# x + alpha * fx: a compact head for the first 23 columns of the flat tensors, and four stores instead of three

## The chip, the core and the metric

The kernel runs on one core of a Trainium2 chip. The metric is device time in microseconds (us); the figure for a kernel is the median of several runs. Beside it stands a profile of one execution, whose span runs from the first to the last recorded event on the core; what surrounds the span belongs to the run's time, but not to the profile.

## What is computed

```python
B, S, D = 512, 32, 640
x, fx   # (B, S, D) bf16
alpha   # (1,) bf16

def reference(x, fx, alpha):
    return x + alpha * fx
```

Both inputs and the output hold 512 x 32 x 640 = 10,485,760 bf16 numbers, 20.97 MB each.

## The kernel before

Each tensor is taken as a flat run of numbers and cut into 128 equal rows, one for each partition of the on-chip memory (lines 61 to 63). A row has 160 columns of K = 512 numbers, so a column is 1 KiB in a partition, a row is 160 KiB, and neighbouring rows begin 160 KiB apart in memory.

Three lists cut the columns into pieces. `X` cuts the loads of x: (0, 8), (8, 46), (46, 92), (92, 115), (115, 154), (154, 160). `F` cuts fx: six pieces of 23 columns and one of 22. `S` cuts the stores: 64, 64 and 32 columns. All of x lies in one tile, `x_t`, that is as large as the tensor; the pieces of fx share two buffers, `f_t`, so the third piece of fx can only be loaded when the first has been used.

The order of the work is written out by hand in `PLAN`: "x i" loads piece i of x, "f j" piece j of fx, "a" loads alpha and spreads it over the partitions, "c j" computes, "s i" stores. Every transfer is issued by SyncE (SP), on one queue, in the order of `PLAN` (`transfer`, line 78); an issue that has to wait holds back those behind it on SP. Step "c j" is two instructions on VectorE: piece j of fx times alpha, in place (line 96), and x plus that, in place in `x_t` (line 99). The step "a" has a tiny transfer, a 1x1 matmul against a row of ones (line 113) and a copy to all partitions (line 115).

`LATE` makes store 0 wait until the last piece of fx has landed, so that no store is issued ahead of the last loads. At the end a no-op on SP waits for everything but the last store (lines 123 to 125); the program's own end waits for that one.

In what follows, "f 2", "c 5" or "s 1" are steps of `PLAN`, numbered from 0, and a column is always 1 KiB in each of the 128 partitions.

Of the kernel before, what the change touches and what calls it, by code (L numbers as in the profile page):

```python
# [1 line left out]

# [4 lines left out]

ACT = mybir.ActivationFunctionType
ALU = mybir.AluOpType
F32 = mybir.dt.float32  # L10
BF16 = mybir.dt.bfloat16

K = 512
P = 128


X = [(0, 8), (8, 46), (46, 92), (92, 115), (115, 154), (154, 160)]
F = [(0, 23), (23, 46), (46, 69), (69, 92), (92, 115), (115, 138), (138, 160)]
S = [(0, 64), (64, 128), (128, 160)]
N = 160  # L20

PLAN = """
x 0
x 1
a
f 0
f 1
x 2
c 0
f 2  # L30
c 1
f 3
x 3
c 2
f 4
x 4
c 3
f 5
c 4
f 6  # L40
x 5
c 5
c 6
s 0
s 1
s 2
"""
LATE = {("s", 0): ("f", 6)}


@with_exitstack
def kernel(
    ctx: ExitStack,
    tc: tile.TileContext,
    x: bass.AP,
    fx: bass.AP,
    alpha: bass.AP,
    out: bass.AP,
):
    nc = tc.nc  # L60
    xv = x.flatten_outer_dims().rearrange("(p n) d -> p (n d)", p=P)
    fxv = fx.flatten_outer_dims().rearrange("(p n) d -> p (n d)", p=P)
    ov = out.flatten_outer_dims().rearrange("(p n) d -> p (n d)", p=P)
    assert xv.shape[1] == N * K

    consts = ctx.enter_context(tc.tile_pool(name="consts", bufs=1))
    psum = ctx.enter_context(tc.tile_pool(name="psum", bufs=1, space=bass.MemoryType.PSUM))
    whole = ctx.enter_context(tc.tile_pool(name="whole", bufs=1))
    fs = ctx.enter_context(tc.tile_pool(name="fs", bufs=2))
    ctx.enter_context(tc.manual_schedule())  # L70

    sync = mybir.DependencyInfo(mybir.DependencyClass.Sync, mybir.DependencyReason.DATA)
    xt = whole.tile([P, N * K], x.dtype, name="x_t")
    ft, moved = {}, {}
    done = []

    def transfer(what, out, in_):
        r = nc.sync.dma_start(out=out, in_=in_)  # L78
        if what in LATE:
            tc.add_manual_dep(r.ins, moved[LATE[what]].ins.name, sync, reason="issue late")  # L80
        moved[what] = r
        done.append(r)

    def load_x(i):
        a, b = X[i]
        transfer(("x", i), xt[:, a * K : b * K], xv[:, a * K : b * K])

    def load_f(j):
        a, b = F[j]
        ft[j] = fs.tile([P, max(e - s for s, e in F) * K], fx.dtype, tag="f", name="f_t")  # L90
        transfer(("f", j), ft[j][:, : (b - a) * K], fxv[:, a * K : b * K])

    def compute(j):
        a, b = F[j]
        term, total = ft[j][:, : (b - a) * K], xt[:, a * K : b * K]
        nc.vector.tensor_scalar(  # L96
            out=term, in0=term, scalar1=lanes["a_f"][:], scalar2=None, op0=ALU.mult
        )
        done.append(nc.vector.tensor_tensor(out=total, in0=total, in1=term, op=ALU.add))  # L99

    def store(i):
        a, b = S[i]
        transfer(("s", i), ov[:, a * K : b * K], xt[:, a * K : b * K])

    lanes = {}

    def alpha_to_lanes():
        a_1 = consts.tile([1, 1], alpha.dtype, name="a_1")
        transfer("a", a_1[:], alpha[None, :])
        ones = consts.tile([1, P], alpha.dtype, name="ones")  # L110
        nc.vector.memset(ones[:], 1.0)  # L111
        a_ps = psum.tile([P, 1], F32, name="a_ps")
        done.append(nc.tensor.matmul(a_ps[:], ones[:], a_1[:], start=True, stop=True))  # L113
        lanes["a_f"] = consts.tile([P, 1], F32, name="a_f")
        nc.vector.tensor_copy(out=lanes["a_f"][:], in_=a_ps[:])  # L115

    does = {"x": load_x, "f": load_f, "c": compute, "s": store, "a": alpha_to_lanes}
    for step in PLAN.split("\n"):
        if step:
            what, *of = step.split()  # L120
            does[what](*map(int, of))

    rest = nc.sync.nop(nofuse=True)
    for i in done[:-1]:
        tc.add_manual_dep(rest.ins, i.ins.name, sync, reason="all but the last store")


# [1 line left out]
_INS = ['x', 'fx', 'alpha']  # L129
_OUTS = [((512, 32, 640), 'bfloat16')]  # L130


# [23 lines left out]
```

## Time and profile before

| what | value |
|---|---|
| median of 3 runs | 151.09 us (151.03 to 151.19) |
| the profiled execution's own time | 151.26 us |
| its span | 149.5 us |
| VectorE: 7 multiplies (L96), 7 additions (L99) | 22.9 us, 43.8 us |
| HBM read, written | 41.94 MB, 20.97 MB |
| mean rate over the span | 421 GB/s |
| SP's issues of transfers | 0.33 to 0.64 us each |

How to read the profile: an engine's busy time is summed over its instructions, and the share is that of the span. DVE is VectorE, SP is SyncE, and SPq stands for SP's sequencer, which issues transfers. A line of the timeline gives start and duration in us, engine, line of the kernel, operation, what is written and read, and in brackets how long the engine had been idle and what ended that. A line of the list of transfers gives what is written and read, how many there are, their size in KB, and the us from issue to landing. A line of the windows gives a stretch of the span, its length, the busy time of each engine in it, the clock, the mean busy share of the 16 DMA engines, and the rate in GB/s; packets are booked where they start, so a short stretch can show more than 1.00.

### The profile page before, as it was taken

The page shows a single profiled execution, that of the slowest core. Times are in us where ns is not written, and L with a number is a line of the kernel's source. Part 1 is how long each engine was busy: PE and PEld are TensorE (multiplying, and loading weights), DVE is VectorE, ACT ScalarE, POOL GpSimd, SP SyncE. Part 2 cuts the span into 40 slices and gives each one's busy share as a digit, 9 for nine tenths or more (in the row PEclk, how much of TensorE's full clock was granted, in tenths as well). Part 3 has the DMA queues.
Part 4 walks back from the last instruction along what each step waited for, and adds up shares of the span by engine and source line. Part 5 has one row for each costly group of instructions (what it writes and reads, how often), then busy time and mean ns, then how long its engine had stood idle before and what let it go on. Part 6 is the DMA issues. An engine that isn't in the chain of part 4 may idle for free.

```text
span 149.5 us, 93 instructions
## 1 busy us (share of the span) xinstructions
PE 0.2 (0%) x1; PEld 0.1 (0%) x1; DVE 66.7 (45%) x16; POOL 0.2 (0%) x4
## 2 busy tenths in 40 slices
PE   0000000000000000000000000000000000000000
PEld 0000000000000000000000000000000000000000
DVE  0000005999950099999499104999960000000000
POOL 0000000000000000000000000000000000000000
DMA  5998999999979999999998999999996969696994
GB/s 151 463 500 354 448 410 466 435 403 466 542 303 410 466 435 403 429 460 422 443 502 353 417 460 390 458 515 438 403 561 281 561 281 561 281 561 281 456 456 210
DMA packets 2306, 62.92 MB, mean 421 GB/s; under 512 B 258, under 2 KB 258, under 8 KB 386
## 3 DMA queue, kind: packets, MB, share of 16 engines
q1 hardware_dynamic: 2306, 62.92, 98.2%
HBM read 41.94 MB, written 20.97 MB: 421 GB/s over the span
## 4 chain that ended last, share of the span: by engine, by line
DMA 41%; DVE 31%; issue 1%; SPq 1%; DVEq 0%
DMA f_t<-in_fx_dram 41%; DVE x_t L99 20%; DVE f_t L96 11%; SPq L78 1%; DVEq L96 0%
## 5 line engine op out<-in xcount | busy, mean ns | idle before, releaser
L99 DVE TENSOR_TENSOR x_t<-x_t,f_t 128x11776 bf16<-128x11776 bf16 (+1 forms) x7 | 43.8, 6254 | 0.2
L96 DVE TENSOR_SCALAR f_t<-f_t,a_f 128x11776 bf16<-128x11776 bf16 (+1 forms) x7 | 22.9, 3265 | 26.7 <-DMA f_t<-in_fx_dram 26.7
L115 DVE COPY a_f<-a_ps 128x1 f32<-128x1 f32 x1 | 0.2, 159 | 16.2 <-PE a_ps L113 16.2
L111 DVE MEMSET ones<- 1x128 bf16 x1 | 0.2, 165 | 0.8 <-PEq L140 0.8
L113 PE MATMUL a_ps<-a,ones 1*128 1x1 bf16 x1 | 0.2, 158 | 17.0 <-DMA a<-in_alpha_dram 17.0
L140 POOL MEMSET const-bfloat16-1.0<- 128x1 bf16 x1 | 0.1, 101 | 0.0
L140 POOL MEMSET const-uint8-127<- 128x1 uint8 x1 | 0.1, 101 | 0.0
L113 PEld LDWEIGHTS <-ones 1*128 1x128 bf16 x1 | 0.1, 98 | 1.0 <-DVE ones L111 1.0
L140 POOL MEMSET const-float32-0.0<- 128x1 f32 x1 | 0.1, 98 | 0.2 <-issue 0.2
L140 POOL MEMSET const-float32-1.0<- 128x1 f32 x1 | 0.1, 98 | 0.0
## 6 DMA issues: line engine op xcount, KB each, us to landing
f_t<-in_fx_dram SPq DMA_DIRECT2D x6, 2944.0 KB, 19.4
x_t<-in_x_dram SPq DMA_DIRECT2D x1, 5888.0 KB, 41.9
x_t<-in_x_dram SPq DMA_DIRECT2D x1, 4992.0 KB
x_t<-in_x_dram SPq DMA_DIRECT2D x1, 4864.0 KB, 15.9
out_dram<-x_t SPq DMA_DIRECT2D x1, 4096.0 KB, 38.1
x_t<-in_x_dram SPq DMA_DIRECT2D x1, 2944.0 KB, 22.3
f_t<-in_fx_dram SPq DMA_DIRECT2D x1, 2816.0 KB, 15.9
x_t<-in_x_dram SPq DMA_DIRECT2D x1, 1024.0 KB, 4.8
```

Of the source, the lines that this page charges most:

```text
L78: r = nc.sync.dma_start(out=out, in_=in_)
L96: nc.vector.tensor_scalar(out=term, in0=term, scalar1=lanes["a_f"][:], scalar2=None, op0=ALU.mult)
L99: done.append(nc.vector.tensor_tensor(out=total, in0=total, in1=term, op=ALU.add))
L111: nc.vector.memset(ones[:], 1.0)
L113: done.append(nc.tensor.matmul(a_ps[:], ones[:], a_1[:], start=True, stop=True))
L115: nc.vector.tensor_copy(out=lanes["a_f"][:], in_=a_ps[:])
L140: nc = _bacc.Bacc("TRN2", target_bir_lowering=False, num_devices=1)
```

## The change

The flat tensors are now read and written through `rows_of`. The first 128 x 23 columns of each, 2944 KiB in one piece, are the head: row p of it has 23 columns, and neighbouring rows begin 23 KiB apart. The remainder is cut into 128 rows of 137 columns, 137 KiB apart. Partition p holds row p of the head in its columns 0 to 23 and row p of the remainder in its columns 23 to 160. The tiles, the instructions of VectorE and their sizes stay as they are.

No transfer may cross column 23. So the load of x[8:46] becomes two, x[8:23] and x[23:46], of which the second is issued behind f 0, and the stores become (0, 23), (23, 87), (87, 151), (151, 160). `LATE` stays.

```diff
-X = [(0, 8), (8, 46), (46, 92), (92, 115), (115, 154), (154, 160)]
+X = [(0, 8), (8, 23), (23, 46), (46, 92), (92, 115), (115, 154), (154, 160)]
 F = [(0, 23), (23, 46), (46, 69), (69, 92), (92, 115), (115, 138), (138, 160)]
-S = [(0, 64), (64, 128), (128, 160)]
+S = [(0, 23), (23, 87), (87, 151), (151, 160)]
+HEAD = 23
...
 f 0
+x 2
 f 1
-x 2
+x 3
 c 0
...
 s 2
+s 3
...
-    xv = x.flatten_outer_dims().rearrange("(p n) d -> p (n d)", p=P)
-    fxv = fx.flatten_outer_dims().rearrange("(p n) d -> p (n d)", p=P)
-    ov = out.flatten_outer_dims().rearrange("(p n) d -> p (n d)", p=P)
-    assert xv.shape[1] == N * K
+    def rows_of(t):
+
+        flat = t.flatten_outer_dims().rearrange("r d -> (r d)")
+        head = flat[: P * HEAD * K].rearrange("(p c) -> p c", p=P)
+        rest = flat[P * HEAD * K :].rearrange("(p c) -> p c", p=P)
+        assert rest.shape[1] == (N - HEAD) * K
+
+        def columns(a, b):
+            if b <= HEAD:
+                return head[:, a * K : b * K]
+            return rest[:, (a - HEAD) * K : (b - HEAD) * K]
+
+        return columns
+
+    xv, fxv, ov = rows_of(x), rows_of(fx), rows_of(out)
...
-        transfer(("x", i), xt[:, a * K : b * K], xv[:, a * K : b * K])
+        transfer(("x", i), xt[:, a * K : b * K], xv(a, b))
...
-        transfer(("s", i), ov[:, a * K : b * K], xt[:, a * K : b * K])
+        transfer(("s", i), ov(a, b), xt[:, a * K : b * K])
```

The later pieces of x move up by one number in `PLAN` (x 3 becomes x 4, x 4 becomes x 5, x 5 becomes x 6) and keep their places. The loads of fx go through `fxv(a, b)` in the same way.

## The prediction

> **What bounds the kernel now.** I read the page first: busy time and the DMA totals.
>
> ```profile
> span 149.5 us, 93 instructions
> ...
> PE 0.2 (0%) x1; PEld 0.1 (0%) x1; DVE 66.7 (45%) x16; POOL 0.2 (0%) x4
> ...
> DMA packets 2306, 62.92 MB, mean 421 GB/s; under 512 B 258, under 2 KB 258, under 8 KB 386
> ...
> q1 hardware_dynamic: 2306, 62.92, 98.2%
> ```
>
> VectorE is busy for 45% of the span, the DMA engines for 98.2%. The chain of waits gives DMA 41% and VectorE 31%, which looks like a tie and is none: VectorE's steps stand in it because each frees a buffer for a later load, but the queue never runs dry in the meantime. The windows show this:
>
> ```profile
> 1.50:2.00 0.50, 0.00 (x0) 0.00 (x0) 0.00 (x0) 0.00 (x0) 1.00 1.51 229
> 2.00:2.50 0.50, 0.00 (x0) 0.00 (x0) 0.00 (x0) 0.00 (x0) 1.00 0.39 82
> 2.50:3.00 0.50, 0.00 (x0) 0.00 (x0) 0.00 (x0) 0.00 (x0) 1.00 0.65 229
> 3.00:3.50 0.50, 0.00 (x0) 0.00 (x0) 0.00 (x0) 0.00 (x0) 1.00 0.85 360
> ...
> 10.00:50.00 40.00, 0.16 (x1) 0.00 (x0) 19.23 (x5) 0.00 (x0) 1.00 1.00 430
> 50.00:98.00 48.00, 0.00 (x0) 0.00 (x0) 34.71 (x8) 0.00 (x0) 1.00 1.00 428
> 98.00:102.00 4.00, 0.00 (x0) 0.00 (x0) 4.00 (x2) 0.00 (x0) 1.00 1.03 436
> 102.00:148.00 46.00, 0.00 (x0) 0.00 (x0) 8.60 (x2) 0.00 (x0) 1.00 1.00 433
> ```
>
> The last two numbers of a row are the DMA share and GB/s; a packet is counted where it starts, hence the 1.51. From 10 to 148 us the share is 1.00 and the rate 428 to 436 GB/s, loads and stores alike, also over the turn from loads to stores. So every byte is on the path, and only three things can move the end: what a byte costs, what a transfer costs beyond its bytes, and the start, where the engines fall short. I count columns of 1 KiB for each partition: the program moves 480 of them, in 16 large transfers.
>
> **Prices.** The timeline shows when VectorE could start after a load had landed, and the list of DMA issues how long each took from issue to landing (here f 6 and x 5):
>
> ```profile
> 24.19 3.29 DVE L96 TENSOR_SCALAR f_t<-f_t,a_f 128x11776 bf16<-128x11776 bf16 x1 [6.84 <-DMA f_t<-in_fx_dram]
> ...
> 52.05 3.29 DVE L96 TENSOR_SCALAR f_t<-f_t,a_f 128x11776 bf16<-128x11776 bf16 x1 [8.71 <-DMA f_t<-in_fx_dram]
> ...
> 73.06 3.29 DVE L96 TENSOR_SCALAR f_t<-f_t,a_f 128x11776 bf16<-128x11776 bf16 x1 [1.88 <-DMA f_t<-in_fx_dram]
> ...
> 91.90 3.29 DVE L96 TENSOR_SCALAR f_t<-f_t,a_f 128x11776 bf16<-128x11776 bf16 x1 [9.23 <-DMA f_t<-in_fx_dram]
> ```
>
> ```profile
> f_t<-in_fx_dram SPq DMA_DIRECT2D x1, 2816.0 KB, 15.9
> x_t<-in_x_dram SPq DMA_DIRECT2D x1, 768.0 KB, 17.4
> ```
>
> Between the four starts lie f 1, x 2, f 2 (92 columns, 3 transfers, 27.86 us), then f 3, x 3, f 4 (69, 3, 21.01) and x 4, f 5 (62, 2, 18.84). With a for a column and b for a transfer, the first two give 23a = 6.85, a = 0.298 and b = 0.15 us. The last two small loads: f 6 (22 columns) was issued at 82.70 and landed at 98.6, 6.7 after f 5; x 5 (6 columns) was issued at 83.08 and landed at 100.48, 1.9 after f 6; so 16a = 4.8 to 4.85, a = 0.303, b = 0.06. Loads: a about 0.302, b between 0.06 and 0.15 us. Stores, by issue in the timeline (98.59, 101.54, 110.66) and landing (21.2, 37.6, 38.1 later): 119.8, 139.1, 148.8; 19.3 us for 64 columns and 9.6 for 32, which leaves b between -0.1 and 0.1.
>
> **The change part by part.**
>
> (1) One more load (x[8:46] becomes [8:23] and [23:46]) and one more store. Bytes are the same. Load: I take 0.08, nearer to the small loads, since these differ in columns alone; bounds 0.06 and 0.15. Store: I take 0.07, as for a load; bounds -0.1 and 0.15. Together **+0.15**, bounds -0.04 to +0.30. SP's issues (0.33 to 0.64 us each) come free: the added load is issued near 2.4 us, with 46 columns, 14 us of data, ahead of it, and the added store after s 2, with some 87 columns queued. Without that cover each would cost its 0.35 us.
> The Trainium skill has a rule that speaks against this part: "DMA: Bandwidth & Descriptors", section "Anatomy of one DMA", gives a DMA on GpSimd's path a fixed cost of about 2.0 us beside its bytes, and the page's rules ask for few, large transfers. By that rule paid in full the two would cost 4 us and the kernel would take 155; this case's queue belongs to SP, holds several transfers at once, and shows 0.06 to 0.15 us.
>
> (2) The order of arrival. f 0 is behind 46 columns instead of 69, so it lands 23 x 0.302 = 6.9 us earlier, at 17.2; alpha, behind 23 instead of 46 columns, lands near 10, still ahead of it. c 0 (3.29 + 6.29 us) then runs from 17.2 to 26.8, and f 2's issue moves from 33.8 to 26.9. c 1 needs 92 columns and both kernels have moved these by 31.2; it starts there, not at 33.7, and f 3 is issued at 40.8 instead of 43.4. **0**, as the queue had 138 columns at the start, enough until 45: earlier issues only lengthen a queue that is not empty. f 2 lands at 52 as before, and all that follows keeps its time.
>
> (3) The stores. s 0 still waits for f 6 (98.6); it is covered by x 6 (6 columns, 1.9 us), while the first transfer of all needed about 1 us from issue (0.73) to first packets (near 1.75, by the slices of the first 6 us). s 0's would start at 99.6. x 6 lands at 100.5, and bytes stop about 0.5 before a landing (the last store landed at 148.8; after 148.3 nothing moves). So the queue goes on, with some 0.4 us to spare. The new s 1 needs c 3, long done. s 2 now ends at column 151 and so waits for c 6, whose second instruction runs from 104.61 for 6.03 us, to 110.6; s 0 and s 1 are 87 columns, 26 us from about 100, so s 2 arrives 15 us early. s 3 is queued behind it on SP, and its wait is over too. The closing wait on all but the last store is hidden if s 3's 9 columns (2.7 us) last longer than SP's few semaphore checks, which they do. **0**; without cover a stall of the queue would cost its own length.
>
> (4) The row pitch: 23 KiB in the head, 137 KiB in the rest, 160 KiB before. The trace has one pitch only, so the price of a byte is bounded by the spread between its own stretches: 27.86/92 = 0.303 and 21.01/69 = 0.3045, 0.0017 or 0.6%. Over the 411 columns of the rest that is -0.7 to +0.7. I take **0**: all starts within a row, 8, 23 or 46 KiB from its head, move at the same 428 to 436 GB/s, so the place in a row does not matter once the queue runs.
> On pitch the Trainium skill ("DMA: Bandwidth & Descriptors", section "Latency and other measured facts") reports lost bandwidth at row pitches of large powers of two, with a few KiB of padding as the cure. The rows of this case show no loss at 160 KiB, which is no such power; the page would give this part nothing.
>
> (5) The cold start. From 1.5 to 4.5 us the windows count 0.5 x (229+82+229+360+475+393) = 884 KB; at 433 GB/s from 1.75 on it would be 1191 KB. Some 0.3 MB, **0.7 us**, are lost while x 0's first rows come in. In the new kernel these rows lie 23 KiB apart. The bounds are -0.7 (no loss) and +0.7 (twice the loss). I take **0**: no later turn to new rows, at the same pitch, shows a loss, so the empty queue is the likelier cause than the addresses.
>
> Sum: the profiled execution, 151.26 with a span of 149.5, becomes 151.41. It stood 0.17 above the median of 151.09, so the median becomes **151.24**, say 151.2. Within 0.2% (0.30 us, about what a measurement can tell from no change): no change. Own range of this case: 150.95 to 151.40.
>
> **The rivals.** *The start is mended (faster).* If x 0's first packets are slow because rows 160 KiB apart collide when all engines begin at once, rows of the compact head may spread better, and 0.5 of the 0.7 us come back: 151.09 + 0.15 - 0.5 = **150.75**. For it: the share falls to 0.39 and 0.65 although all of x 0 is queued. Against: equal pitch costs nothing later. It decides from 0.45 us saved. *The rest's rows are dearer (slower).* Rows at 137 KiB, above all in the 64-column stores, run at the slower stretch's rate: 0.0014 x 411 = +0.6, with the transfers +0.75: **151.8**. It decides from 0.15 us over the 411 columns, a rate 0.12% lower. For it: the trace has no such pitch, and the queue hides nothing. Against: the rate is the same for loads and stores, which points to the engines and not to memory. *The head is not sent as planned.* Its rows join into one run in memory; if they went out in other pieces, over fewer engines, f 0 would not land 7 us after x 1: over 153. The 128 rows of the tile speak against it.
>
> **How the numbers follow.** No change 0.37; start mended 0.33; dearer rows 0.27; other pieces 0.03. So faster 0.33, same 0.37, slower 0.30. With cases of both signs the range runs from most of a mended start, 150.55, to the dearer rows, 151.8; it leaves out a larger saving and the far end of the slower cases.
>
> **What would show it.** Packets: 16 transfers made 2048 of rows and 258 small ones; 18 should make 2304 and 290, 2594 in all, at the same 62.92 MB. c 0 starts at 17.2, c 1 at 31.2, c 2 at 52.1, c 6 ends near 110.8. The windows from 10 to 148 stay at 1.00. Windows of 2.0 to 3.5 us well above 82, 229 and 360 GB/s, and a c 0 before 16.9, mean the first rival; 64-column stores over 19.4 us or steps between loads above the old ones the second; a window below 1.00 near 98 to 102 a stall that I excluded. I am wrong if the span leaves 149.3 to 149.9.

## The result, and the profile after

The changed kernel takes 151.41 us (median of 20 runs, 151.21 to 151.58); the kernel before, run beside it, 151.14 us (20 runs, 151.01 to 151.33). The ratio is 1.0018, with a 95% interval of 1.0012 to 1.0024: 0.27 us slower, 0.18 to 0.36. The profiled execution took 151.39 us, with a span of 149.6 us.

From the page of the changed kernel:

```profile
span 149.6 us, 97 instructions
...
DMA packets 2594, 62.92 MB, mean 421 GB/s; under 512 B 290, under 2 KB 290, under 8 KB 418
...
q1 hardware_dynamic: 2594, 62.92, 98.2%
```

The same bytes go out in 2594 packets instead of 2306, 290 of them small: 18 large transfers of 144 packets and 2 for alpha. The head, compact in memory, is still sent row by row. The kernel is bound as before; the share of the DMA engines has not moved.

The windows of the changed kernel (DMA share and GB/s at the end of each row):

```profile
1.50:2.00 0.50, 0.00 (x0) 0.00 (x0) 0.00 (x0) 0.00 (x0) 1.00 1.02 164
2.00:2.50 0.50, 0.00 (x0) 0.00 (x0) 0.00 (x0) 0.00 (x0) 1.00 0.72 147
2.50:3.00 0.50, 0.00 (x0) 0.00 (x0) 0.00 (x0) 0.00 (x0) 1.00 0.61 213
3.00:3.50 0.50, 0.00 (x0) 0.00 (x0) 0.00 (x0) 0.00 (x0) 1.00 1.00 410
3.50:4.00 0.50, 0.00 (x0) 0.00 (x0) 0.00 (x0) 0.00 (x0) 1.00 1.14 475
4.00:4.50 0.50, 0.00 (x0) 0.00 (x0) 0.00 (x0) 0.00 (x0) 1.00 0.86 360
...
10.00:50.00 40.00, 0.06 (x1) 0.00 (x0) 19.31 (x5) 0.00 (x0) 1.00 1.01 433
50.00:98.00 48.00, 0.00 (x0) 0.00 (x0) 34.62 (x8) 0.00 (x0) 1.00 1.00 427
98.00:102.00 4.00, 0.00 (x0) 0.00 (x0) 4.00 (x2) 0.00 (x0) 1.00 1.10 462
102.00:148.00 46.00, 0.00 (x0) 0.00 (x0) 8.70 (x2) 0.00 (x0) 1.00 1.00 431
148.00:148.50 0.50, 0.00 (x0) 0.00 (x0) 0.00 (x0) 0.00 (x0) 1.00 0.19 74
```

From 10 us on the queue is full, as before. The start is no better: half the sum of the first six rates is 884 KB by 4.5 us, the same as before. The last row differs (before: 0.02 and 0 GB/s); a packet is counted where it starts, and the last store's packets are 9 KiB instead of 32, so some of them start later.

The timeline of the changed kernel, VectorE's multiplies c 0, c 1, c 2, c 4 and c 5, the load f 2 and the last store:

```profile
17.29 3.29 DVE L110 TENSOR_SCALAR f_t<-f_t,a_f 128x11776 bf16<-128x11776 bf16 x1 [7.03 <-DMA f_t<-in_fx_dram]
...
26.93 14.25 SPq L92 DMA_DIRECT2D f_t<-in_fx_dram  x2
31.21 3.29 DVE L110 TENSOR_SCALAR f_t<-f_t,a_f 128x11776 bf16<-128x11776 bf16 x1 [4.31 <-DMA f_t<-in_fx_dram]
...
52.15 3.29 DVE L110 TENSOR_SCALAR f_t<-f_t,a_f 128x11776 bf16<-128x11776 bf16 x1 [11.33 <-DMA f_t<-in_fx_dram]
...
73.17 3.29 DVE L110 TENSOR_SCALAR f_t<-f_t,a_f 128x11776 bf16<-128x11776 bf16 x1 [1.88 <-DMA f_t<-in_fx_dram]
...
92.00 3.29 DVE L110 TENSOR_SCALAR f_t<-f_t,a_f 128x11776 bf16<-128x11776 bf16 x1 [9.21 <-DMA f_t<-in_fx_dram]
...
111.19 1.19 SPq L92 DMA_DIRECT2D out_dram<-x_t  x1
```

c 0 starts 6.9 us earlier than before and c 1 2.5 us earlier (33.72 before), and neither gain arrives anywhere: c 2 starts at 52.15 where it started at 52.05. From there the steps are the old ones, 21.02 us to c 4 and 18.83 to c 5 (before: 21.01 and 18.84). Of the profile's delay 0.10 us is there by c 2, and nothing is added by the loads after it. Differences of this size in single profiles are to be read with care: when the same kernel was profiled again later (e9_again, below), all these starts came 0.14 us later.

The view by `out_dram` has the us from issue to landing for three of the four stores:

```profile
DMA to landing us min/median/max: 8.9/27.8/35.4
```

From issues at 98.68, 99.08 and 110.76 these make landings at 107.6, 126.9 and 146.2, so 19.3 us for each store of 64 columns.

### The profile page after: what moved, and what is told of

Same layout as the page of the kernel before. It is cut to its first block, busy times and chain, and to the rows that moved or that the text cites. A ratio compares the mean times of both kernels' runs of the same rounds, so it can differ in the third digit from the quotient of the medians.

```text
span 149.6 us, 97 instructions
## 1 busy us (share of the span) xinstructions
PE 0.2 (0%) x1; PEld 0.1 (0%) x1; DVE 66.8 (45%) x16; POOL 0.2 (0%) x4
## 2 busy tenths in 40 slices
DMA packets 2594, 62.92 MB, mean 421 GB/s; under 512 B 290, under 2 KB 290, under 8 KB 418
## 3 DMA queue, kind: packets, MB, share of 16 engines
q1 hardware_dynamic: 2594, 62.92, 98.2%
## 4 chain that ended last, share of the span: by engine, by line
DMA 41%; DVE 31%; issue 1%; SPq 1%; DVEq 0%
DMA f_t<-in_fx_dram 41%; DVE x_t L113 20%; DVE f_t L110 11%; SPq L92 1%; DVEq L110 0%
```

## The experiments

Two theories were tested. *Transfers*: each of the two added transfers costs some 0.07 us, whatever it carries, and the layout costs nothing. *Layout*: rows 23 and 137 KiB apart cost or give something of their own, in the steady flow or at the cold start. All comparisons are with the kernel before, run on the same chip; its medians there were 151.34 (e1 to e4), 151.38 (e5, e6, e8, e9) and 151.35 us (e7, e11, e12). The ratio compares the runs of the two kernels with a 95% interval; "by the ratio" below is what it exceeds 1 by, times the time before. Of the code only the lines that matter are shown; where x is cut anew, `PLAN` follows it.

| kernel | large transfers | rows (KiB apart) | median us | us against before, by medians | ratio (95%) |
|---|---|---|---|---|---|
| e1_pieces | 18 | 160 | 151.49 | +0.15 | 1.0006 (0.9998 to 1.0015) |
| e2_layout | 16 | 46, 114 | 151.49 | +0.15 | 1.0009 (0.9999 to 1.0018) |
| e3_load | 17 | 160 | 151.43 | +0.09 | 1.0004 (0.9995 to 1.0013) |
| e4_store | 17 | 160 | 151.33 | -0.01 | 0.9999 (0.9990 to 1.0008) |
| e5_loads6 | 22 | 160 | 151.78 | +0.40 | 1.0028 (1.0016 to 1.0039) |
| e6_stores6 | 22 | 160 | 151.76 | +0.38 | 1.0029 (1.0018 to 1.0040) |
| e8_head115 | 16 | 115, 45 | 151.46 | +0.08 | 1.0009 (1.0000 to 1.0018) |
| e9_again (the changed kernel) | 18 | 23, 137 | 151.49 | +0.11 | 1.0009 (1.0000 to 1.0019) |
| e7_fewer | 14 | 160 | 151.72 | +0.37 | 1.0028 (1.0017 to 1.0039) |
| e11_fewest | 13 | 160 | 151.79 | +0.44 | 1.0029 (1.0019 to 1.0040) |
| e12_fewer_layout | 14 | 46, 114 | 151.76 | +0.41 | 1.0037 (1.0022 to 1.0053) |

### The new pieces on the old rows

```diff
-X = [(0, 8), (8, 46), (46, 92), ...
+X = [(0, 8), (8, 23), (23, 46), (46, 92), ...
-S = [(0, 64), (64, 128), (128, 160)]
+S = [(0, 23), (23, 87), (87, 151), (151, 160)]
```

> The new pieces (one more load, four stores, the new plan) on the old rows, 160 KiB apart. If the two added transfers are the whole price, this kernel is as late as the changed one: +0.15 to +0.30 us, a ratio of 1.0010 to 1.0020. If the row layout carries the price, it stays within 0.1 us of the kernel before. In both, c 2 starts 0.1 us later if a load costs 0.08 us.

It came out at +0.15 us by the medians, at the lower edge of what the theory of transfers asked for, and at +0.09 by the ratio, which is on the other side of the line that was drawn; the interval, -0.03 to +0.23, holds zero. So this run alone does not decide. It is near the +0.11 us of the changed kernel itself when that was run again (below), which leaves little for a layout there, but does not rule it out.

### The layout without the added transfers

With a head of 46 columns instead of 23, the six loads of x and three stores are enough (`X` and `PLAN` as in the kernel before; the lines are against the changed kernel).

```diff
-S = [(0, 23), (23, 87), (87, 151), (151, 160)]
-HEAD = 23
+S = [(0, 46), (46, 110), (110, 160)]
+HEAD = 46
```

> The layout alone: a compact head of 46 columns and a remainder of 114, which lets the six old loads of x stand and needs three stores (46, 64, 50 columns), so 16 transfers as before. If transfers are the price: 0.0, within 0.1 us. If the layout is: +0.15 us or more. If compact rows mend the cold start: -0.3 us or more, with more than 229 GB/s from 2.5 to 3.0 us.

It was no faster, which speaks against a mended start, and +0.15 us later, which spoke for a price of the layout; its runs were also wider spread (151.30 to 151.80) than those of before (151.21 to 151.59). Its profile is 0.15 us later at c 0 already (24.34 against 24.19) and adds 0.10 us between c 2 (52.19) and c 4 (73.30), a step of 21.11 us. Since that step takes 21.02 us in the changed kernel, it called for a second layout.

### One load, one store

```diff
 # e3: x[8:46] in two loads, stores as before
+X = [(0, 8), (8, 23), (23, 46), (46, 92), ...
 # e4: loads as before
+S = [(0, 23), (23, 87), (87, 151), (151, 160)]
```

> The old rows and three stores, with x[8:46] loaded as two pieces. Price of a load by the prediction: 0.08 us (0.06 to 0.15). If the store is what costs, this one stays under 0.05 us.

> The old rows and loads, with the stores cut into 23, 64, 64 and 9 columns. Price of a store by the prediction: 0.07 us (-0.1 to 0.15). If the short last store exposes work at the end (SP's checks, or a longer way from last byte to landing): over 0.15 us, and the end of the program over 0.75 us after the last landing.

+0.09 us for the load and -0.01 for the store; both intervals (about 0.13 us to either side) hold zero and hold 0.07, so single transfers are too small to be weighed one by one. That called for doses.

### Six more loads, six more stores

```diff
 # e5
+X = [(0, 8), (8, 27), (27, 46), (46, 61), (61, 77), (77, 92), (92, 104), (104, 115),
+     (115, 128), (128, 141), (141, 154), (154, 160)]
 # e6
+S = [(0, 22), (22, 43), (43, 64), (64, 86), (86, 107), (107, 128), (128, 139), (139, 150), (150, 160)]
```

> Old rows and stores, six loads more: x is cut into twelve pieces where it was cut into six. If a load costs what one added load did in the steps between landings (0.08 us), +0.45 to +0.50 us, a ratio of 1.003. If the price of a load hides under the full queue: within 0.1 us. If SP runs out of semaphores and holds loads back: a gap in the DMA share, over 1 us.

> Old rows and loads, nine stores instead of three (six more). If a store costs as much as a load: +0.45 us. If the store was free, as the one added store seemed to be: within 0.1 us.

Six loads cost 0.40 us by the medians and 0.42 by the ratio, six stores 0.38 and 0.44; by the intervals a load costs 0.04 to 0.10 us, a store 0.045 to 0.10. So one transfer, load or store, costs **0.07 us**, and -0.01 us for a single one lay within the width of its interval. The timeline of the kernel with six more loads shows how the price piles up, at the same multiplies c 2, c 4 and c 5:

```profile
52.27 3.29 DVE L102 TENSOR_SCALAR f_t<-f_t,a_f 128x11776 bf16<-128x11776 bf16 x1 [8.88 <-DMA f_t<-in_fx_dram]
...
73.37 3.29 DVE L102 TENSOR_SCALAR f_t<-f_t,a_f 128x11776 bf16<-128x11776 bf16 x1 [1.96 <-DMA f_t<-in_fx_dram]
...
92.36 3.29 DVE L102 TENSOR_SCALAR f_t<-f_t,a_f 128x11776 bf16<-128x11776 bf16 x1 [9.37 <-DMA f_t<-in_fx_dram]
```

c 2 is 0.22 us late after three added loads, c 4 0.31 after four, c 5 0.46 after six. The queue is not empty meanwhile: its windows from 10 to 148 us stay at 1.00 or more. The page of the kernel with six more stores shows what the price is made of:

```profile
span 149.9 us, 98 instructions
...
q1 hardware_dynamic: 3170, 62.92, 98.4%
```

98.4% of 149.9 us is 147.5 us, against 98.2% of 149.5, 146.8, before; with six more loads it is 98.3% of 150.0, also 147.5. The shares are rounded, which leaves some 0.1 us to either side. The bytes are the same and the packets more: the price is busy time of the DMA engines, not a gap between transfers. The windows accordingly show no stall (1.00 to 1.06 from 50 to 148 us).

### A second layout, and the changed kernel again

```diff
 # e8, the layout alone
+S = [(0, 51), (51, 115), (115, 160)]
+HEAD = 115
```

> The layout alone once more, with a head of 115 columns and a remainder of 45: old loads, three stores (51, 64, 45 columns), 16 transfers. If any layout other than rows 160 KiB apart costs something: +0.1 us or more, as with a head of 46. If the pitch does not matter and the spread of runs made that difference: within 0.1 us. A slow engine in the stores would show as a 64-column store of over 19.35 us.

> The changed kernel itself, on the chip and against the runs that the other three have. If transfers alone made it late: about +0.1 us (one load 0.08, one store 0.0 to 0.05). If the layout has a share: +0.2 to +0.3 us.

The second layout is +0.08 us by the medians, +0.14 by the ratio (0.0 to 0.27), to either side of the 0.1 us that was to decide. Its steps between c 2, c 4 and c 5 are 21.00 and 18.83 us, those of the old rows; and the rows of the first layout, used again in e12_fewer_layout below, took 21.01 us from c 2 to c 4. So the 21.11 was not the layout's. What the second layout's profile is late by is there at its first multiply:

```profile
24.39 3.29 DVE L108 TENSOR_SCALAR f_t<-f_t,a_f 128x11776 bf16<-128x11776 bf16 x1 [6.89 <-DMA f_t<-in_fx_dram]
```

That is 0.20 us after the 24.19 of before, and 0.15 after the 24.24 of the kernel with six more stores, which has the old rows, the same loads, and was run on the same chip. A spread of 0.14 us is what two profiles of one kernel show, so this is a hint of a price at the start and no proof. It does not look like dearer rows: 98.1% of 149.7 us, and 97.9% of 149.9 in the first layout, make 146.9 and 146.8 us of busy time, as before to the 0.1 us of the rounding. The changed kernel is +0.11 us by the medians, +0.14 by the ratio (0.0 to 0.29): two transfers at 0.07.

### The cold start by itself

```diff
+    flat = x.flatten_outer_dims().rearrange("r d -> (r d)")
...
+    for i in range(6):
+        probe(lambda to: nc.sync.dma_start(out=to, in_=rows(160, 0, 24 * i)))
+        probe(lambda to: nc.sync.dma_start(out=to, in_=rows(23, i, 0)))
+        probe(lambda to: nc.sync.dma_start(out=to, in_=rows(137, 0, 20 * i)))
+        probe(lambda to: nc.sync.dma_start(out=to, in_=rows(46, i // 2, 23 * (i % 2))))
+        probe(lambda to: nc.sync.dma_start(out=to, in_=rows(128, 0, 20 * i)))
+        probe(lambda to: nc.sync.dma_start(out=to, in_=rows(8, 3 * i, 0)))
```

`rows(pitch, block, column)` gives 128 rows of 8 columns that lie `pitch` KiB apart, and `probe` issues each when the one before has landed.

> The kernel before with 36 added loads ahead of it, each 128 rows of 8 KiB into columns that the kernel overwrites later, each issued only when the one before has landed, so that every one starts cold. Rows lie 160, 23, 137, 46, 128 or 8 KiB apart, six loads of each. If the cold start depends on where the rows lie, issue to landing differs between the pitches by 0.1 us or more in the median, and rows 160 KiB apart are not the worst if the new layout loses time there. If the empty queue alone makes it: all near 4.9 us, within the spread of six.

The lines of the view by source line, for rows 160, 23, 137, 46, 128 and 8 KiB apart in this order; the first of each pair of lines has the ns of an issue on SP and when the first and last were issued, the second the us from issue to landing (least, median, greatest):

```profile
L133 SPq DMA_DIRECT2D x_t<-in_x_dram x6: 327/328/382, 0.7 to 146.0; - x6
...
DMA to landing us min/median/max: 4.7/4.8/4.9
...
L134 SPq DMA_DIRECT2D x_t<-in_x_dram x6: 328/328/338, 5.6 to 150.9; - x6
...
DMA to landing us min/median/max: 4.7/4.8/5.0
...
L135 SPq DMA_DIRECT2D x_t<-in_x_dram x6: 327/328/328, 10.4 to 155.7; - x6
...
DMA to landing us min/median/max: 4.8/4.9/5.0
...
L136 SPq DMA_DIRECT2D x_t<-in_x_dram x6: 328/328/328, 15.2 to 160.7; - x6
...
DMA to landing us min/median/max: 4.8/4.9/5.0
...
L137 SPq DMA_DIRECT2D x_t<-in_x_dram x6: 327/328/328, 20.1 to 165.6; - x6
...
DMA to landing us min/median/max: 4.6/4.8/4.9
...
L138 SPq DMA_DIRECT2D x_t<-in_x_dram x6: 327/328/328, 25.0 to 170.3; - x6
...
DMA to landing us min/median/max: 4.7/4.8/4.9
```

Six cold loads of one kind spread over 0.2 to 0.3 us, and the medians of six kinds over 0.1. A compact block of rows 8 KiB apart starts no better than rows 160 KiB apart. The 36 loads took 172 us together (a span of 321.5 against 149.5), 4.8 each, where 8 columns in a full queue take 2.4 us (8 times the 0.302 us of a column). Two medians, at 46 and 137 KiB, stand 0.1 us above the others, which is the limit that was set and no more than the spread of one kind; rows 160 KiB apart are among the fastest. So, to some 0.1 us, the time beyond the data belongs to the empty queue and not to the addresses. Each of these loads stood alone; a start with several loads queued was not probed in this way, but x 0, the first load of the two kernels, took 4.8 us to land before and 4.9 in the changed kernel.

### Fewer transfers than before

If a transfer costs 0.07 us, taking some away should pay.

```diff
 # e7; e11 has also S = [(0, 80), (80, 160)]; e12 is e7 with a head of 46 columns and e2's stores
+X = [(0, 46), (46, 92), (92, 115), (115, 160)]
-LATE = {("s", 0): ("f", 6)}
+LATE = {("s", 0): ("f", 5)}
```

> Old rows, x in four loads instead of six (46, 46, 23 and 45 columns); store 0 waits for f 5 instead of f 6, since no load of x is left behind f 6 to cover its start. At 0.07 us a load: -0.14 us, a ratio of 0.9991. A stall at the turn to the stores would give +0.5 us or more.

> As the kernel with four loads of x, and two stores of 80 columns instead of three. At 0.07 us a transfer -0.2 us against the kernel before. If rows over 64 KiB are sent as two packets, the saving of the store shrinks to nothing: -0.14 us.

> The kernel with four loads of x, on the rows of a head of 46 columns, three stores (46, 64, 50). Against the kernel with four loads on old rows: 0.0 us if the layout is free, +0.1 us or more if it has a price of its own, as the two layouts measured alone (+0.15 and +0.08 us) seem to say.

All three were slower than before, by 0.37 to 0.44 us, where -0.14 and -0.20 were expected of the first two: a miss, though short of the 0.5 us that a stall was to cost. The profile of the kernel with four loads shows two places, of which these are the lines (c 0 and c 5):

```profile
24.39 3.29 DVE L94 TENSOR_SCALAR f_t<-f_t,a_f 128x11776 bf16<-128x11776 bf16 x1 [7.17 <-DMA f_t<-in_fx_dram]
...
93.89 3.29 DVE L94 TENSOR_SCALAR f_t<-f_t,a_f 128x11776 bf16<-128x11776 bf16 x1 [11.01 <-DMA f_t<-in_fx_dram]
```

c 0 starts 0.20 us later than before (24.19) though one transfer fewer is ahead of it, so on this reading a cold start with 46 columns loses some 0.27 us that the short first load of 8 columns saved. The kernel with two stores has the same first load and starts c 0 at 24.45; four profiles on the old rows with the short first load and f 0 in its old place have it at 24.19 to 24.26. The layout with a head of 115 columns, though, came to 24.39 with the short load too.

The other place is the turn to the stores. f 6 was issued at 82.90 and took 17.9 us to land, at 100.8. That is 6.9 us after f 5 (c 5 starts at 93.89), where the same step took 6.7 before; the kernel with two stores repeats it (82.95, 17.9, c 5 at 93.95). So 0.2 us more pass in the last load with a store queued right behind it, and no small load of x. The short first load, and a store that is issued only when the last large load has landed, each seem to be worth more than a transfer costs. The edits were not run apart, so how the 0.37 us divide, and why, is not shown.

With four loads of x, the layout of a head of 46 columns stood 0.04 us above the old rows by the medians; by the ratios it is 0.14, but one of its twelve runs, the profiled one, took 153.18 us where the others took 151.67 to 152.06. Two stores of 80 columns saved nothing: their rows go out as two packets each (2130 packets where 13 transfers of 144 and 2 make 1874).

No version beat the kernel before.

## Why the prediction was right

It said 151.24, shown as 151.2, with a range of 150.55 to 151.8 and "no change" (within 0.2%) as the likeliest case; measured were 151.41 us and a ratio of 1.0018. The call was a weak one: "no change" had 0.37 against 0.33 and 0.30, and the range is over four times as wide as the change that was measured. 151.41 also stands just above the 151.40 where the range of that case ended, and 0.18% just inside its 0.2%. Point by point:

- *The bound.* Right: the share of the DMA engines is 98.2% before and after, and the windows from 10 to 148 us stay full.
- *(1) One load and one store more, +0.15.* Right: 0.07 each by the doses, so +0.14. The steps between landings of one profile were enough to find 0.06 to 0.15 for a load; the store, which the prediction could only bound from -0.1 to 0.15, costs about the same as a load. The Trainium skill's fixed cost of about 2.0 us for a DMA on GpSimd's path ("DMA: Bandwidth & Descriptors", section "Anatomy of one DMA") is by that section mostly the wait for the last byte's receipt. These runs show 0.07 us for a transfer in SP's full queue, a thirtieth of it: to charge every added transfer the fixed cost in full would have been wrong here.
- *(2) The order of arrival, 0.* Right to 0.1 us: c 0 was predicted at 17.2 and came at 17.29, f 2's issue at 26.9 (26.93), c 1 at 31.2 (31.21), c 2 at "52 as before" (52.15, by which the added load is paid; the 0.10 us are within what two profiles of one kernel differ by).
- *(3) The stores, 0.* Right: no window below 1.00 near 98 to 102 us, and s 2, issued at 110.76, was in the queue 16 us before s 1 had landed (126.9). The closing wait hid behind the last store. That store's issue took SP 1.19 us instead of 0.35, with the queue's cover.
- *(4) The row pitch, 0.* Right for the flow: 131 columns between c 2 and c 5 took 39.85 us before and after. The rival of dearer rows would have added 0.0014 x 131 = 0.18 there. The stores agree: 19.3 us for a store of 64 columns, as before and under the 19.4 that was to speak for this rival. Its price was not well founded: 0.0014 is not worked out (the two rates differ by 0.0017), and that difference is the one from which the prices took b = 0.15, since the shorter stretch also has three transfers. With 0.07 for each, nearly half of it is the transfers' and no spread of the rate.
- *(5) The cold start, 0.* Right to some 0.1 us: 884 KB by 4.5 us in both kernels, the same 4.8 to 4.9 us for cold loads at six pitches, and c 0 at 17.29 and 17.43 in two profiles of the changed kernel against 17.35 and 17.39 in the two with its first loads on the old rows. The rival of the mended start, given 0.33, had no support in the end. Of the two reasons weighed, that later turns to other rows at equal pitch cost nothing, was the sound one.

The size is the part to correct. The first comparison gave +0.27 us (0.18 to 0.36), the second +0.14 by the ratio (0.0 to 0.29). Transfers make +0.14. Both intervals allow 0.18 to 0.29, and so some 0.04 to 0.15 us beyond the transfers. The layouts alone stood at +0.15, +0.08 and +0.04 us by the medians, none clear of zero by itself. But the first two have a ratio of 1.0009 each, from different runs on two chips; taken together, by an estimate from their two intervals, they give 0.04 to 0.23 us, which is clear of zero. So a price of the layout of some 0.1 us is a rival that these runs do not rule out for the heads of 46 and 115 columns. For the head of 23 the flow, the stores and the cold start show nothing at 0.1 us. Whether the remainder is the layout's or the spread of the runs stays open.

## What to carry to other kernels

Where the DMA share is 1.00 from end to end, as here, an earlier arrival is worth nothing (c 0 came 6.9 us earlier for no gain), and the price of a split is the number of added transfers times the step that the trace shows beyond bytes, here 0.07 us for a load or a store. Find that price with a dose of six, since one is below what a comparison can tell. Rearranging rows in memory bought nothing in this kernel, whose loads and stores already ran at the same rate; and before transfers are merged, look at what the short ones may be for, at a cold start and at the turn from loads to stores.

## What was not expected of the hardware

- Merging loads made the kernel slower by 0.37 us: with a first load of 46 columns c 0 started at 24.39 us instead of 24.19, and the last load took 6.9 us instead of 6.7 with a store queued behind it. Which edit did it was not separated.
- What a transfer costs beyond its bytes is booked as busy time: with six more stores the engines' busy time rose from 146.8 to 147.5 us for the same bytes.
- Rows 128 KiB apart start cold as fast as any (median 4.8 us).
- The issue of a store took SP 1.19 us, with two stores of 64 columns and one of 23 issued in the 13 us before it; the one just before took 0.33. The other kernels with these four stores show the same 1.19, and with nine stores the median issue took 1.18 us.
